# Reordered products, new tiles for exponentials and later operand splits in a softmax-attention and Fourier-mixing kernel

## The chip, the cores and the metric

The kernel runs on 1 core of one Trainium2 chip. The metric is the device time of one execution in microseconds (us); the time before is the median of 3 runs.

## The reference, cut to what matters

One input x of 2048 rows and 512 columns goes through 32-head softmax attention (a head has 16 columns) and through a Fourier mixing layer, and a gate per row mixes the two:

```python
x = A_x                                              # [1, 2048, 512]
g = sigmoid((x * gate_w).sum(-1, keepdims=True))
q, k, v = split(x @ wqkv)                            # 32 heads of 16
p = softmax(q k^T / 4)                               # 2048 x 2048 for each head
a = concat(p @ v) @ wo
re, im = x @ dft_hid_re.T, x @ dft_hid_im.T
b = dft_seq_re @ re - dft_seq_im @ im
out = g * a + (1 - g) * b
```

All inputs and outputs are float32.

## The kernel before, in words

The kernel is one long program whose order is written out by hand: every engine executes its instructions in the order in which the Python code emits them.

**Number formats.** Products that need full precision are made of three single-pass products: an operand is split into a high and a low half (`hi`, `lo`, type float32r), and high x high, high x low and low x high are summed in PSUM. Scores use stacked rows of such halves: a product of 48 or 50 rows holds them all.

**Two halves of the rows.** Nearly all products contract over 64 rows or fewer, so that two run side by side in TensorE, one on rows 0 to 63 (`j = 0`) and one on rows 64 to 127 (`j = 1`). The two heads of a pair lie on the two halves. A product in the lists below is a letter and the half: `e1` is an `e` on rows 64 to 127.

**The front** (to about 345 us) makes q, k, v, the gate and the two halves of the hidden transform (`ab_d`, kept in DRAM), and begins to scan scores for their maxima.

**The main part** is 512 steps, in 256 rounds of two steps. A step belongs to a pair of heads, a half of the queries (1024 columns) and a block of 128 keys. In a round TensorE executes products of four kinds:

- `e` (L633, `score`): a score product into a PSUM bank, read by the exponential on ScalarE (L621, `exponentials`), which writes a tile of 128 x 512 in SBUF. There are 8 in a round.
- `c` (L664, `scan`): a score product of a later pair of heads into a PSUM bank, read by a maximum on VectorE (L666). There are 6 in most rounds.
- `s` (L882, `fill` and `emit`): a filler, one of the products of the Fourier layer's sequence transform (`spectral`), and after it of the output projection (`mix_heads`, `mix_some`). Each half has a bank of its own for them (`z0`, `z1`); when a group of products is complete, VectorE takes it out (L791, L793, L827 `take_in`).
- the weighted values of two earlier steps (L643, `pv`), which use all 128 rows and read 4 exponential tiles per step.

**Order and banks.** `ORDERS` holds the order of the products in a round, by the number of scan pairs and of fillers per half: `(3, 8)` is the usual one. In rounds 0 to 41 (`SINGLES`) there are no fillers, and each half of a round uses `ORDERS[1]`. `e` and `c` share PSUM banks, seven in rounds 0 to 41 and five (`b0` to `b4`) after. Which bank a product gets is decided at build time by the class `Banks`, a small model of the two halves, of ScalarE and of VectorE: it hands out the bank that is free first by its own reckoning. Its constants are in ns.

**Exponential tiles.** There are 17 places of 128 x 512 (`unused`). Before the change they are 17 fixed tiles, 8 of them parts of the `ring4` tiles (named `eb`), 9 of their own (`e`), which are written again and again. `pv` gives the places of its step back.

**Work in the other queues.** VectorE, ScalarE, GpSimd (POOL) and the SP queue of DMAs execute their instructions in order too:

- `split_unit` (L231, L232, POOL) splits a unit of sequence coefficients into `chi` and `clo`, operands of the next 12 fillers of each half.
- `part_b` splits the imaginary part of the hidden transform, one block of 128 rows at a time, into the halves `oh` and `ol` (L928, L929, POOL), and stores them (L933, SP). Two blocks are done in every 16 steps; all are done within the first 128 steps.
- At the end of every 16 steps, `quotients` copies the weighted values out of PSUM (L673, VectorE), and `divide` turns them, in three pieces at later rounds, into halves: `invert` (L683, L684), `spread` (L688) and `scale` (L691 to L699, POOL, into tiles that are also tagged `oh` and `ol`, stored by L706).
- `output_operands` loads and splits the output matrix, one piece at each `next(operands)`: the split is a cast and a subtraction on VectorE (L740, L741).

Of the kernel before, what the change touches and what calls it, by code (L numbers as in the profile page):

```python
# [10 lines left out]
F32 = mybir.dt.float32  # L11
# [7 lines left out]
P = 128  # L19
# [8 lines left out]
VC = DH + 1  # L28
# [31 lines left out]
def build(tc, x, xT, wqkv, wo, wrT, wiT, cr, ci, gate, out):  # L60
    nc = tc.nc
    with ExitStack() as ctx:
# [4 lines left out]
        ring4 = ctx.enter_context(tc.tile_pool(name="ring4", bufs=4, reuse_waits="tile"))  # L67
# [170 lines left out]
        with ExitStack() as px:  # L238
# [125 lines left out]
            if True:  # L364
                wb = px.enter_context(tc.tile_pool(name="wb", bufs=1))
# [195 lines left out]
        with ExitStack() as pa:  # L561
# [23 lines left out]
            class Banks:  # L585

                slot, late, gap, load, group = 230.0, 450.0, 106.0, 200.0, 854.0
                period, release = {"e": 480.0, "c": 680.0}, {"e": 760.0, "c": 860.0}
                names = [f"b{i}" for i in range(5)] + ["z0", "z1"]

                def __init__(self):
                    self.t, self.rows, self.free = 0.0, [0.0, 0.0], [0.0] * 7
                    self.count = 7
                    self.engine, self.values = {"e": 0.0, "c": 0.0}, False

                def take(self, kind, j):
                    if self.values:
                        self.t += self.load
                        self.rows, self.values = [self.t, self.t], False
                    s = max(self.t, self.rows[j])  # L600
                    if kind != "s":
                        b = min(range(self.count), key=lambda b: self.free[b])
                        s = max(s, self.free[b])
                        a = max(self.engine[kind], s + self.late)
                        self.engine[kind], self.free[b] = a + self.period[kind], a + self.release[kind]
                    self.t, self.rows[j] = s + 4.0, s + self.slot
# [503 lines left out]
```

## Time and profile before

| | |
|---|---|
| median of 3 runs | 1775.72 us (1775.24 to 1777.4) |
| the profiled execution's own time | 1774.39 us |
| its span | 1772.6 us, mean clock 0.99 |
| DVE (VectorE) busy | 1259.0 us, 71% |
| ACT (ScalarE) busy | 1328.3 us, 75% |
| POOL (GpSimd) busy | 671.3 us, 38% |
| DMA | 207.01 MB, mean 117 GB/s |

The costliest groups (line, engine, operation, tiles, count; busy us, mean ns) are these:

| group | busy, mean |
|---|---|
| L666 DVE maxima x1312 | 858.0 us, 686 ns |
| L621 ACT exponentials x2048, in two groups | 587.1 and 529.3 us, 638 and 637 ns |
| L633 PE score products x2048 | 685.5 us, 417 ns |
| L882 PE fillers, chi x2060 | 556.2 us, 396 ns |
| L664 PE scan products x1312 | 554.3 us, 456 ns |

Times are those of one profiled execution. PE is TensorE's products, PEld its weight loads. Two products that run side by side are both counted as busy, and so is one that waits for its bank, so that the sums of busy time are larger than the time that TensorE needs. Neighbouring ACT instructions overlap in the trace: their starts are closer together than one lasts. A line of the order of time gives the start, the length, the engine, the line, the operation, the tiles, the shapes and how many instructions were merged; behind it, in brackets, stands the idle time before it and what ended that.

### The profile page before, as it was taken

The page shows a single profiled execution, that of the slowest core. Times are in us where ns is not written, and L with a number is a line of the kernel's source. Part 1 is how long each engine was busy: PE and PEld are TensorE (multiplying, and loading weights), DVE is VectorE, ACT ScalarE, POOL GpSimd, SP SyncE. Part 2 cuts the span into 40 slices and gives each one's busy share as a digit, 9 for nine tenths or more (in the row PEclk, how much of TensorE's full clock was granted, in tenths as well). Part 3 has the DMA queues.
Part 4 walks back from the last instruction along what each step waited for, and adds up shares of the span by engine and source line. Part 5 has one row for each costly group of instructions (what it writes and reads, how often), then busy time and mean ns, then how long its engine had stood idle before and what let it go on. Part 6 is the DMA issues. An engine that isn't in the chain of part 4 may idle for free.

```text
span 1772.6 us, 37250 instructions
## 1 busy us (share of the span) xinstructions
PE 1732.2 (98%) x13657; PEld 1076.3 (61%) x13657; DVE 1259.0 (71%) x2385; ACT 1328.3 (75%) x2589; POOL 671.3 (38%) x828
## 2 busy tenths in 40 slices
PE   8999999999999999999999999999999999999898
PEld 6777788744445565666566665566556656655454
DVE  5599899766676677777777767777777777776334
ACT  5589988799986677777777767677777777777685
POOL 0264210533434544444444444434434444442122
PEclk9999999999999999999999999999999999999999
DMA  7575335763444252333332265524342524426512
GB/s 260 188 235 157 84 118 141 197 174 90 107 108 115 83 144 64 83 96 82 77 93 80 68 180 171 130 63 100 96 100 64 133 58 97 110 58 186 140 42 99
DMA packets 135176, 207.01 MB, mean 117 GB/s; under 512 B 56192, under 2 KB 58736, under 8 KB 130672
## 3 DMA queue, kind: packets, MB, share of 16 engines
q1 hardware_dynamic: 94320, 176.24, 35.6%
q0 software_dynamic: 38496, 19.47, 4.8%
q10 hardware_dynamic: 2176, 8.92, 1.8%
q8 instruction: 107, 1.75, 0.4%
q14 instruction: 77, 0.63, 0.1%
HBM read 138.28 MB, written 65.81 MB: 115 GB/s over the span
## 4 chain that ended last, share of the span: by engine, by line
PE 88%; DMA 4%; issue 2%; DVE 1%; POOL 1%; ACT 1%; SPq 1%; DVEq 0%; POOLq 0%; ACTq 0%
PE pvb L643 26%; PE z L882 23%; PE s L664 12%; PE s L633 12%; PE xy L320 6%; PE s L173 5%; PE xy L336 4%; DMA o_d<-ol 1%; DMA lc<-ob 1%; POOL lc L676 1%; SPq L127 0%; DMA q_d<-el 0%; DMA ks<-k_d 0%; DVE y L827 0%; DVE ob L673 0%
## 5 line engine op out<-in xcount | busy, mean ns | idle before, releaser
L666 DVE TENSOR_REDUCE mx<-s 128x1 f32<-128x512 f32 x1312 | 858.0, 686 | 302.9 <-PE s L633 227.5
L621 ACT ACTIVATE e<-s 128x512 f32<-128x512 f32 x1081 | 587.1, 638 | 182.1 <-PE s L633 167.3
L633 PE MATMUL s<-qs,ks 50*128 50x512 f32 x2048 | 685.5, 417 | 5.1 <-DVE mx L666 4.3
L621 ACT ACTIVATE eb<-s 128x512 f32<-128x512 f32 x967 | 529.3, 637 | 170.2 <-PE s L633 145.2
L882 PE MATMUL z<-b,chi 64*128 64x512 f32 x2060 | 556.2, 396 | 6.2 <-POOL chi L231 6.2
L664 PE MATMUL s<-ks,qs 48*128 48x512 f32 x1312 | 554.3, 456 | 0.0
L633 PEld LDWEIGHTS s<-qs,ks 50*128 50x128 f32 x2048 | 349.1, 186 | 148.9 <-issue 71.2
L643 PE MATMUL pvb<-e,va 128*17 128x512 f32 x2162 | 407.7, 595 | 0.0
L643 PE MATMUL pvb<-eb,va 128*17 128x512 f32 x1934 | 379.6, 597 | 0.0
L882 PEld LDWEIGHTS z<-b,chi 64*128 64x128 f32 x2060 | 342.5, 188 | 36.5 <-POOL chi L231 6.9
L882 PE MATMUL z<-b,clo 64*128 64x512 f32 x1030 | 346.8, 396 | 0.3 <-POOL clo L232 0.3
L664 PEld LDWEIGHTS s<-ks,qs 48*128 48x128 f32 x1312 | 229.3, 185 | 179.4 <-ACT e L621 82.5
L179 DVE CUSTOM_DVE_ANT_0 fold<-s,fold 128x512 f32<-128x512 f32 x368 | 242.7, 689 | 25.3 <-ACT fold L177 8.7
L173 PE MATMUL s<-ks,qs 48*128 48x512 f32 x736 | 231.9, 400 | 1.5 <-ACT fold L177 1.1
L231 POOL CAST chi<-craw 128x512 fp32r<-128x512 f32 x126 | 77.5, 615 | 393.2 <-PE z L882 393.0
L177 ACT ACTIVATE fold<-s 128x512 f32<-128x512 f32 x368 | 203.4, 605 | 28.3 <-PE s L173 27.1
L882 PEld LDWEIGHTS z<-b,clo 64*128 64x128 f32 x1030 | 180.8, 188 | 16.9 <-POOL clo L232 1.6
L232 POOL TENSOR_TENSOR clo<-craw,chi 128x512 fp32r<-128x512 f32 x126 | 162.1, 1286 | 10.7 <-PE z L882 0.3
L676 POOL DMA_DIRECT2D lc<-ob x124 | 63.4, 516 | 251.2 <-DVE ob L673 249.4
L173 PEld LDWEIGHTS s<-ks,qs 48*128 48x128 f32 x736 | 133.8, 184 | 35.8 <-DVE mx L179 12.8
L643 PEld LDWEIGHTS pvb<-e,va 128*17 128x17 f32 x2162 | 70.3, 96 | 112.5 <-issue 111.8
L643 PEld LDWEIGHTS pvb<-eb,va 128*17 128x17 f32 x1934 | 64.8, 96 | 98.5 <-issue 98.0
(129 smaller groups left out, 1756.5 us busy)
## 6 DMA issues: line engine op xcount, KB each, us to landing
craw<-cr SPq DMA_DIRECT2D x64, 256.0 KB
craw<-ci SPq DMA_DIRECT2D x64, 256.0 KB
ks<-k_d SPq DMA_DIRECT2D x54, 256.0 KB
qs<-q_d SPq DMA_DIRECT2D x66, 128.0 KB
ab_d<-ab SPq DMA_DIRECT2D x32, 256.0 KB
y_d<-y SPq DMA_DIRECT2D x32, 256.0 KB
b<-bs_d SPq DMA_DIRECT2D x32, 256.0 KB
o_d<-oh POOLq DMA_DIRECT2D x28, 256.0 KB, 9.5
```

The lines of the kernel that those rows point to most:

```text
L173: nc.tensor.matmul(ps, qs[b:b + 48, qb * P:(qb + 1) * P], ks[b:b + 48, c * 512:(c + 1) * 512], start=True, stop=True)
L177: seen_by(nc.scalar.activation(fold[j], ps, AF.Relu))
L179: seen_by(nc.vector.tensor_tensor_reduce(out=fold[j], in0=ps, in1=fold[j], scale=1.0, scalar=-3.0e38, op0=ALU.add, op1=ALU.max, accum_out= ...
L232: sub(lo, raw, hi.bitcast(F32))
L320: ins = nc.tensor.matmul(ps, lhs[64:P], rhs[64:P], start=False, stop=last)
L621: nc.scalar.activation(e, ps, AF.Exp, scale=SCALE)
L633: nc.tensor.matmul(ps, ks[b:b + 50, kb * P:(kb + 1) * P], qs[b:b + 50, q0:q0 + 512], start=True, stop=True)
L643: nc.tensor.matmul(pvb[r:r + VC, :], va[:, kb, 2 * p + j, :], es[step][c, j], start=kb == 0, stop=kb == NB - 1, tile_position=(0, r))
L664: nc.tensor.matmul(ps, qs[b:b + 48, qb * P:(qb + 1) * P], ks[b:b + 48, c * 512:(c + 1) * 512], start=True, stop=True)
L666: nc.vector.tensor_reduce(mx[p][:, j, qb, c:c + 1], ps, axis=AX.X, op=ALU.max)
L676: nc.gpsimd.dma_start(lc[32 * n:32 * n + 32, :], ob[r + DH:r + VC, :].rearrange("p (s e) -> p s e", e=16))
L882: nc.tensor.matmul(ps, pr_.lhs(j), pr_.rhs(j), start=group.count[j] == 1, stop=group.count[j] == group.size)
```

## The change

The change has five parts.

- Most entries of `ORDERS` have the same products in another order.
- An exponential writes a new tile, taken from the pool `pr` under one of 17 tags, where it wrote one of 17 fixed tiles. The `ring4` pool is closed with the front, and all 17 places lie in `pr`.
- `Banks` has other constants, and its reckoning now has the weight loads (`weights`, one after another through one port) and the swap of weights in each half.
- After the spectral part, each round takes one piece of `output_operands` where it took two.
- In `part_b` a block is split 7 steps after its load where it was 2, and stored 9 steps after it where it was 4; the odd blocks begin one step earlier (3 steps behind the even ones, not 4).

```diff
-    1: "e1 e0 c1 e0 c0 e1",
+    1: "e0 e1 c0 c1 e0 e1",
     0: "e0 e1 e0 e1",
-    (3, 8): "c1 e0 s1 c0 s1 e0 e1 s0 s0 s1 s0 c1 e1 s0 s1 c0 s1 s0 e1 s0 s1 e0 s1 c0 s1 s0 e1 s0 e0 c1",
+    (3, 8): "c0 e1 c0 e1 s0 s1 s0 s1 s0 s1 e0 s1 c0 e1 s1 s0 c1 e0 s1 s0 s1 s0 s0 c1 e1 s0 e0 s1 e0 c1",
...
-    (0, 9): "e1 s0 s1 e0 e1 s0 s1 s0 s1 s0 s1 s0 s1 e0 s1 s0 s1 s0 e1 e0 e1 e0 s1 s0 s1 s0",
-    (0, 6): "e0 e1 e0 s1 s0 s1 s0 s1 s0 e1 e0 e1 s0 s1 e0 s1 s0 s1 s0 e1",
+    (0, 9): "s0 e1 s0 s1 s0 s1 e0 s1 e0 e1 e0 s1 s0 s1 s0 s1 s0 s1 s0 s1 e0 e1 s0 s1 s0 e1",
+    (0, 6): "e0 s1 s0 e1 s0 e1 e0 s1 s0 s1 s0 e1 e0 s1 s0 s1 s0 s1 e0 e1",
...
-        ring4 = ctx.enter_context(tc.tile_pool(name="ring4", bufs=4, reuse_waits="tile"))
...
+                ring4 = px.enter_context(tc.tile_pool(name="ring4", bufs=4, reuse_waits="tile"))
...
-            both = [ring4.tile([P, 2, 512], F32, tag="c", name="eb") for _ in range(4)]
-            unused = [b[:, j, :] for b in both for j in range(2)]
-            unused += [pr.tile([P, 512], F32, name=f"e{i}") for i in range(9)]
+            unused = list(range(17))
...
-                slot, late, gap, load, group = 230.0, 450.0, 106.0, 200.0, 854.0
-                period, release = {"e": 480.0, "c": 680.0}, {"e": 760.0, "c": 860.0}
+                slot, late, gap, load, group, weights, second = 226.0, 425.0, 93.0, 207.0, 854.0, 103.0, 56.0
+                period, release = {"e": 475.0, "c": 682.0}, {"e": 635.0, "c": 735.0}
...
                     if self.values:
-                        self.t += self.load
-                        self.rows, self.values = [self.t, self.t], False
-                    s = max(self.t, self.rows[j])
+                        t = self.t = self.port = self.t + self.load - self.weights
+                        self.rows, self.swap, self.values = [t, t], [t, t + self.second], False
+                    s = max(self.port, self.swap[j])
                     if kind != "s":
                         b = min(range(self.count), key=lambda b: self.free[b])
                         s = max(s, self.free[b])
-                        a = max(self.engine[kind], s + self.late)
-                        self.engine[kind], self.free[b] = a + self.period[kind], a + self.release[kind]
-                    self.t, self.rows[j] = s + 4.0, s + self.slot
-                    return kind != "s" and self.names[b]
+                    self.port = s + self.weights
+                    self.t = self.swap[j] = max(self.port, self.rows[j], self.t + 6.0)
+                    self.rows[j] = self.t + self.slot
+                    if kind == "s":
+                        return None
+                    a = max(self.engine[kind], self.t + self.late)
+                    self.engine[kind], self.free[b] = a + self.period[kind], a + self.release[kind]
+                    return self.names[b]
...
-                    e = es[step][c, j] = unused.pop(0)
+                    i = unused.pop(0)
+                    e = pr.tile([P, 512], F32, tag=f"e{i}", name="e")
+                    es[step][c, j] = e, i
                     nc.scalar.activation(e, ps, AF.Exp, scale=SCALE)
...
-                for s, i in ((2 * s, i), (2 * s + 1, i - 4)):
+                for s, i in ((2 * s, i), (2 * s + 1, i - 3)):
...
-                elif i == 2:
+                elif i == 7:
                     hi, lo = (ap.tile([P, D], F32R, tag=tag, name=tag) for tag in ("oh", "ol"))
...
-                elif i == 4:
+                elif i == 9:
...
                 if m >= OUTM:
-                    for _ in range(2):
-                        next(operands, None)
+                    next(operands, None)
```

More of the change, by code (lines that the diff above doesn't have):

```diff
@@ L585, in build @@
             class Banks:
[L587 to L588 removed]
+                slot, late, gap, load, group, weights, second = 226.0, 425.0, 93.0, 207.0, 854.0, 103.0, 56.0
+                period, release = {"e": 475.0, "c": 682.0}, {"e": 635.0, "c": 735.0}
                 names = [f"b{i}" for i in range(5)] + ["z0", "z1"]
                 def __init__(self):
[L592 to L593 removed]
+                    self.t, self.port, self.rows, self.swap = 0.0, 0.0, [0.0, 0.0], [0.0, 0.0]
+                    self.free, self.count = [0.0] * 7, 7
                     self.engine, self.values = {"e": 0.0, "c": 0.0}, False
@@ L642, in pv @@
                 for c, j, r in quads:
-                    nc.tensor.matmul(pvb[r:r + VC, :], va[:, kb, 2 * p + j, :], es[step][c, j],
+                    nc.tensor.matmul(pvb[r:r + VC, :], va[:, kb, 2 * p + j, :], es[step][c, j][0],
                                      start=kb == 0, stop=kb == NB - 1, tile_position=(0, r))
-                unused.extend(es.pop(step).values())
+                unused.extend(i for e, i in es.pop(step).values())
                 exponentials()
```

4 rows, old and new, of the table ORDERS are left out of this document.

## The prediction

> **What bounds the kernel now.** I read the page first, then the busy time by stage, then single rounds in order of time, and last the waits. The page:
>
> ```profile
> span 1772.6 us, 37250 instructions
> PE 1732.2 (98%) x13657; PEld 1076.3 (61%) x13657; DVE 1259.0 (71%) x2385; ACT 1328.3 (75%) x2589; POOL 671.3 (38%) x828
> PE 88%; DMA 4%; issue 2%; DVE 1%; POOL 1%; ACT 1%; SPq 1%; DVEq 0%; POOLq 0%; ACTq 0%
> ```
>
> TensorE sets the end, but 98% busy does not say that it loses nothing: a product that waits for a bank, beside a running one, still counts as busy. So I go by the length of a round. Exponentials (L621) in the first part (83 half-rounds, rounds 0 to 41) and in the 188 spectral rounds with three scan pairs:
>
> ```profile
> 349.00:512.00 163.00, 162.06 (x332) 0.99 0.48 122
> 524.35:1622.78 1098.43, 781.03 (x1504) 1.00 0.38 98
> ```
>
> The columns are window, length, ACT busy (count), clock. 332 / 4 is 83 half-rounds of 1.96 us, with ScalarE busy 99%: ScalarE is the bound there. 1504 / 8 is 188 rounds of 5.84 us, with ScalarE at 71%: there it is TensorE. One of these (864 to 870), PEld its weight loads:
>
> ```profile
> 863.92 0.49 PE L664 MATMUL s<-ks,qs 48*128 48x512 f32 x1
> 863.93 0.49 PE L633 MATMUL s<-qs,ks 50*128 50x512 f32 x1
> 864.26 0.39 PE L882 MATMUL z<-b,chi 64*128 64x512 f32 x1
> 864.49 0.40 PE L882 MATMUL z<-b,clo 64*128 64x512 f32 x1
> 865.20 0.18 PEld L664 LDWEIGHTS s<-ks,qs 48*128 48x128 f32 x1
> 865.69 0.18 PEld L664 LDWEIGHTS s<-ks,qs 48*128 48x128 f32 x1
> 866.67 0.18 PEld L664 LDWEIGHTS s<-ks,qs 48*128 48x128 f32 x1
> 867.37 0.18 PEld L633 LDWEIGHTS s<-qs,ks 50*128 50x128 f32 x1 [0.17 <-ACT e L621]
> 867.48 0.39 PE L633 MATMUL s<-qs,ks 50*128 50x512 f32 x1
> 867.80 0.62 PE L643 MATMUL pvb<-eb,va 128*17 128x512 f32 x4
> 869.64 0.18 PEld L664 LDWEIGHTS s<-ks,qs 48*128 48x128 f32 x1 [0.85 <-ACT eb L621]
> 864.55 0.60 ACT L621 ACTIVATE e<-s 128x512 f32<-128x512 f32 x1 [1.48 <-PE s L633]
> 865.04 0.59 ACT L621 ACTIVATE e<-s 128x512 f32<-128x512 f32 x1
> 866.23 0.39 PE L633 MATMUL s<-qs,ks 50*128 50x512 f32 x1
> 866.72 0.60 ACT L621 ACTIVATE e<-s 128x512 f32<-128x512 f32 x1
> 864.46 2.56 DVE L666 TENSOR_REDUCE mx<-s 128x1 f32<-128x512 f32 x4 [1.54 <-PE s L633]
> ```
>
> A round is 15 pairs (one product on each half of the rows) and then two steps of weighted values. The first gap between pairs is 0.34, later ones 0.23 (864.26 to 864.49). Free of waits the last pair starts at 0.34 + 13 x 0.231 = 3.34; here the last product starts at 867.48 - 863.92 = 3.56. So 0.22 of this 5.72 us round are waits, and four weight loads show for what: 865.20, 865.69 and 867.37 stand 0.05 behind the end of an exponential (864.55 + 0.60, 865.04 + 0.59, 866.72 + 0.60), 866.67 behind one between them. They wait for a bank that ScalarE still reads. That is the room of the new orders: 0.22 x 188 = 41 us at most. The other 0.12 of the mean 5.84 is a few long waits, below.
>
> **The orders.** I redo the round with the new order, from the rows' constants: an exponential starts 0.62 after the round's first pair, later 0.49 after its product (866.23 to 866.72) or the one before it (864.55 to 865.04), and its bank takes weights 0.65 after that start. A reduction starts 0.54 after the first pair, else 0.61 after the one before ((2.56 - 0.69) / 3), and frees its bank 0.69 later. Weights lead their product by 0.10 (867.37 to 867.48). The new order has c0 e1, c0 e1, three pairs of fillers, e0 s1 (at 1.26), c0 e1 (1.49), fillers, c1 e0 (1.96), two of fillers, then c1 (2.65), e1 (2.88), e0 (3.11) and e0 c1 (3.34). The first five take empty banks. Exponentials free theirs at 1.27, 1.76, 2.40, 2.89, 3.38; reductions at 1.23, 1.84, 2.72, 3.33. In turn: c0 and e1 at 1.49 take 1.23 and 1.27; c1 and e0 at 1.96 take 1.76 and 1.84; c1 at 2.65 takes 2.40; e1 at 2.88 takes 2.72 (its 0.10 of weights fit); e0 at 3.11 takes 2.89; the last pair takes 3.33 and 3.38 and starts at 3.48. Four waits become one: 3.56 - 3.48 = 0.08 a round, 15 us over 188. Where the plan hands out the last two banks in the other order, the end is the same, since both are in one pair. The rounds with nine fillers a side or fewer have no waits to lose: they are 5.05 apart (below), which is 5.72 - 0.22 less two slots.
>
> **New tiles for exponentials.** One line, and four exponentials of the bound first part:
>
> ```profile
> L621 ACTq EVENT_SEMAPHORE  x1031: 17/17/17, 352.0 to 1624.3; - x172
> 426.10 1.35 ACT L621 ACTIVATE eb<-s 128x512 f32<-128x512 f32 x2
> 426.61 0.84 ACT L621 ACTIVATE eb<-s 128x512 f32<-128x512 f32 x1
> 427.10 0.84 ACT L621 ACTIVATE e<-s 128x512 f32<-128x512 f32 x1
> 427.58 1.34 ACT L621 ACTIVATE e<-s 128x512 f32<-128x512 f32 x2
> 428.06 1.35 ACT L621 ACTIVATE e<-s 128x512 f32<-128x512 f32 x2
> ```
>
> Half of the 2048 exponentials have a second wait as an instruction of its own. By the code it is ScalarE's own count, beside TensorE's, because the fixed tile was written by an earlier exponential. Starts stand 0.51, 0.49, 0.48, 0.48 apart: around that wait 0.04 more than two plain ones. A new tile in an old place should wait for its last reader only, which is TensorE again, so one wait is left. In the first part a half-round then takes 4 x 0.48 = 1.92 instead of 163 / 83 = 1.964: 83 x 0.045 = 3.7 us. TensorE's own need there lies below it: before ScalarE is full, half-rounds take 1.88 (from 355.65 to 357.53), so at most 0.08 x 83 = 6.6 us could come, and at least nothing.
>
> ```profile
> 355.65 0.19 PEld L633 LDWEIGHTS s<-qs,ks 50*128 50x128 f32 x2 [0.85 <-issue]
> 357.53 0.19 PEld L633 LDWEIGHTS s<-qs,ks 50*128 50x128 f32 x2 [0.85 <-issue]
> ```
>
> In the spectral rounds each exponential that waits starts about 0.05 earlier (in the first pair the reduction starts after 0.54, the exponential after 0.62). Then the last pair takes 3.33 at worst and starts at 3.43: 0.13 a round instead of 0.08, 188 x 0.13 = 24.4 us. Bounds: 0, where the plan's banks miss, and 41. The Trainium skill (Perfetto Trace Analysis, Identifying Dependency Chains) says that an instruction that waits for several engines may get such a wait put before it. If the second wait were another engine's, a new tile would remove nothing; that is a rival below, and by it the sum is 13 us smaller.
>
> **Output operands.** Rounds after the spectral part, and what DVE did:
>
> ```profile
> 1644.43:1652.80 8.37, 0.81 (x7) 0.49 (x5) 3.15 (x5) 0.60 (x1) 3.64 (x3) 0.82 0.57 105
> 1652.80:1659.42 6.62, 6.62 (x43) 3.82 (x41) 3.22 (x5) 3.75 (x7) 0.00 (x0) 0.71 0.02 4
> 1659.42:1664.47 5.05, 5.05 (x48) 2.79 (x44) 1.50 (x2) 4.13 (x8) 0.00 (x0) 1.00 0.51 110
> 1649.48 0.43 DVE L740 CAST b<-wor 128x512 fp32r<-128x512 f32 x1 [10.17 <-DMA wor<-wo]
> PE z L882 <- DVE y L827: 8.2, 2, 7.6
> ```
>
> The first two lines are one round of 14.99 us; the next takes 5.05. DVE stood 10.17 us in a cast (L740) whose operand had not landed, and behind it the take_in (L827) that frees the z bank. Now the cast is asked for one round after the loads; with one part per round it is two rounds later, 2 x 5.05 = 10.1 us, against the 10.17. Without the stall the operand lands at 1649.5 in the round that starts near 1648.3, and the take_in queued behind is due only at that round's end, 1653: covered. 14.99 - 5.05 = 9.9 us gained; bounds 0 and 10. What else is later (the last split, three rounds) has more than ten rounds before its first use. The clock in the second line (0.71) is part of the price. The Trainium skill (TensorE: Matmul & The Clock Gate, Part 1) has the clock halved after an idle window and restored after 3.4 us busy; by it the stall costs 7.6 + 1.7 = 9.3, the sum 0.6 less. The trace agrees: 9.9, with 0.71 in the round's second half.
>
> **Coefficient halves later.** POOL splits them (L928), in the same queue as the split of the filler's operands (L231):
>
> ```profile
> 518.73 0.86 POOL L706 DMA_DIRECT2D o_d<-oh  x1
> 528.64 0.61 POOL L928 CAST oh<-braw 128x512 fp32r<-128x512 f32 x1 [8.23 <-DMA o_d<-oh]
> 576.11 0.61 POOL L928 CAST oh<-braw 128x512 fp32r<-128x512 f32 x1 [5.18 <-DMA o_d<-oh]
> 530.07:539.91 9.84, 7.71 (x50) 4.33 (x46) 4.12 (x6) 4.45 (x8) 7.46 (x10) 0.83 0.38 122
> 568.79:575.14 6.35, 6.18 (x52) 3.37 (x48) 3.96 (x6) 4.29 (x8) 2.06 (x3) 1.00 0.40 97
> 575.14:586.83 11.69, 7.42 (x52) 4.06 (x48) 3.95 (x6) 4.24 (x8) 7.49 (x10) 0.85 0.27 88
> ```
>
> Against 5.72 these three rounds lose 4.1 + 0.6 + 6.0 = 10.7 us: POOL waits for the store of the quotients' halves to land (9.9 us after issue at 518.73) because both use tile oh, and the filler's split comes late. Only the last steps of this work fall into spectral rounds. Later, the split no longer stands ahead of the quotients' scaling, so that store is issued 2 to 5 us earlier, and the first stall (4.1) goes; the second split meets the landing about 3 us less early. New is a wait at the period's end: the odd half's bs_d store (SP queue) is issued in the very macro in which the scaling asks for oh; POOL stands there some 4 us, with L231 queued behind it. The filler's split has about 1.4 rounds, 8 us, of slack, which covers one such wait and not two. I take +6, bounds -8 and +10.7.
>
> **The sum.** 24.4 + 3.7 + 9.9 + 6 = 44 us. The profiled execution takes 1774.4 (1772.6 span); it would be 1730.4. The median of the runs is 1775.7, 1.3 above it: **1731.7**.
>
> **The rivals.** (1) The second wait stays: rounds gain 0.08, the first part nothing: 15 + 9.9 + 6 = 31, 1744.8. For it: the profile's rows do not name what the wait is for. 0.10. (2) The later splits collide with the scaling: -8 instead of +6, 1745.7. For it: POOL's new wait of 4 us; against: only three periods. 0.08. (3) The orders gain nothing, since banks are handed out by planned times: 19.6 is left, 1756. 0.09. (4) **Slower**: the plan now reckons a bank free 0.425 + 0.635 = 1.06 after an exponential's product, the rows show 0.49 + 0.65 = 1.14 and more. If a product at the round's end is given a bank whose exponential is one further back in the queue, it waits 0.48 more: last pair at 3.91, 0.35 over now, +66 us in all, less the other 19.6: 1822. It decides against the change from 0.10 a round lost on (19.6 / 188). Against it: the hand count has each bank free in the order that the plan assumes. 0.08. The forecast has 0.62; the last 0.03 are gains and losses that cancel.
>
> **How the numbers follow.** A measurement of this kernel can tell about 0.2% (3.6 us). Faster: 0.62 + 0.10 + 0.08 + 0.09 = 0.89, same 0.03, slower 0.08. The range takes in the rivals up to (3), and below the forecast all waits of a round gone (41) with 3.7, 9.9 and 10.7: 65 us, 1710. So 1710 to 1757.
>
> **What would show it.** Right: 1504 exponentials of the spectral rounds in about 1065 us, half-rounds of 1.92, no L621 event semaphores, no long wait of L740, rounds near 1650 of 5.05. Wrong: weight loads still behind exponentials three or four times a round, the event semaphores still there, or new POOL waits in L698 with TensorE behind L231 near 585 and 620.

## The result and the profile after

The changed kernel takes 1753.74 us, the median of 4 runs (1749.17 to 1757.9), against 1775.5 of the kernel before on the same chip (1775.24 to 1777.4): a ratio of 0.9875 (0.9848 to 0.9901). That is 22 us, half of the 44 forecast. The profiled execution took 1752.48 us. Its page, with the lines that answer to those of before:

```profile
span 1750.7 us, 36734 instructions
PE 1717.3 (98%) x13657; PEld 1028.3 (59%) x13657; DVE 1257.5 (72%) x2385; ACT 1346.2 (77%) x2589; POOL 669.9 (38%) x828
PE 81%; DMA 6%; issue 3%; POOL 3%; DVE 2%; SPq 1%; ACT 0%; DVEq 0%; POOLq 0%; ACTq 0%
```

DMA and POOL have grown in the chain that ended last (the work that sets the end, followed back step by step), from 4% to 6% and from 1% to 3%. That is a first hint that TensorE now waits more for data; the rounds below show where. (In this kernel the exponential is L625, the score product L637, the weighted values L647, the scan L668, its maximum L670, the filler L886, its operand's split L230.)

A usual spectral round of it, 872.31 to 877.92, by its score and scan products, the weight load that shows a wait, and the start of the next round:

```profile
872.31 0.49 PE L668 MATMUL s<-ks,qs 48*128 48x512 f32 x1
872.64 0.39 PE L668 MATMUL s<-ks,qs 48*128 48x512 f32 x1
873.58 0.40 PE L637 MATMUL s<-qs,ks 50*128 50x512 f32 x1
873.82 0.39 PE L668 MATMUL s<-ks,qs 48*128 48x512 f32 x1
874.28 0.39 PE L668 MATMUL s<-ks,qs 48*128 48x512 f32 x1
874.98 0.39 PE L668 MATMUL s<-ks,qs 48*128 48x512 f32 x1
875.21 0.39 PE L637 MATMUL s<-qs,ks 50*128 50x512 f32 x1
875.45 0.39 PE L637 MATMUL s<-qs,ks 50*128 50x512 f32 x1
875.64 0.18 PEld L637 LDWEIGHTS s<-qs,ks 50*128 50x128 f32 x1 [0.23 <-ACT e L625]
875.68 0.47 PE L668 MATMUL s<-ks,qs 48*128 48x512 f32 x1
876.08 1.91 PE L647 MATMUL pvb<-e,va 128*17 128x512 f32 x16
877.92 0.50 PE L668 MATMUL s<-ks,qs 48*128 48x512 f32 x1
```

The hand count of the new order had pairs at 1.26, 1.49, 1.96, 2.65, 2.88, 3.11 and the last at 3.43. They stand at 1.27, 1.51, 1.97, 2.67, 2.90, 3.14 and 3.37 behind 872.31. One weight load of the last pair still stands behind an exponential, and the round has next to no wait left. The stages tell what became of it. These are the windows of after for the exponentials of the spectral rounds, and for the rounds around the three longest waits (window, length, the five engines busy, clock, DMA share, GB/s; the first line has ACT alone):

```profile
524.70:1611.30 1086.60, 800.55 (x1504) 0.99 0.38 100
...
570.30:582.30 12.00, 9.23 (x52) 4.36 (x48) 4.05 (x6) 4.45 (x8) 9.34 (x12) 0.72 0.37 122
644.30:655.90 11.60, 8.64 (x50) 5.60 (x46) 4.15 (x6) 4.46 (x8) 1.89 (x2) 0.71 0.64 143
1013.90:1024.60 10.70, 7.55 (x50) 5.20 (x46) 4.15 (x6) 4.46 (x8) 0.00 (x0) 0.84 0.77 181
1646.40:1651.50 5.10, 5.10 (x50) 2.85 (x46) 2.58 (x5) 4.16 (x10) 0.00 (x0) 1.00 0.74 155
```

The 188 rounds take 1086.6 us and not 1098.4. Three of them take 10.7 to 12 us. After the spectral part a round near 1650 takes 5.1; the 14.99 us round is gone.

By stage, from the first products of the rounds (a median round is the median of their distances):

| stage | before | after |
|---|---|---|
| rounds 0 to 41, 83 half-rounds | 166.7 us | 165.7 us |
| the half-round there, median | 1.960 us | 1.960 us |
| rounds 44 to 63 | 125.8 us | 119.7 us |
| rounds 64 to 231 | 972.7 us | 967.0 us |
| median round of these | 5.732 us | 5.611 us |
| rounds 234 to 249 | 92.8 us | 82.6 us |

So 1.0 + 6.1 + 5.7 + 10.2 = 23 us are in these stages. (The first 1.0 is no gain: the first score product comes at 346.64 and not at 345.58.) The median round gained 0.121 us, which would be 20.3 us over the 168 rounds from 64 on; 5.7 came. The question is where the other 14.6 went.

### The profile page after: what moved, and what is told of

The parts are those of the page before. It is cut to its first block, busy times and chain, and to the rows that moved or that the text cites. A ratio compares the mean times of both kernels' runs of the same rounds, so it can differ in the third digit from the quotient of the medians.

```text
span 1750.7 us, 36734 instructions
## 1 busy us (share of the span) xinstructions
PE 1717.3 (98%) x13657; PEld 1028.3 (59%) x13657; DVE 1257.5 (72%) x2385; ACT 1346.2 (77%) x2589; POOL 669.9 (38%) x828
## 4 chain that ended last, share of the span: by engine, by line
PE 81%; DMA 6%; issue 3%; POOL 3%; DVE 2%; SPq 1%; ACT 0%; DVEq 0%; POOLq 0%; ACTq 0%
PE pvb L647 25%; PE z L886 20%; PE s L668 14%; PE s L637 12%; PE xy L319 4%; PE s L172 4%; PE xy L335 3%; POOL el L261 1%; DMA lc<-ob 1%; SPq L126 1%; DMA ks<-k_d 1%; DMA o_d<-ol 1%; DMA qs<-q_d 1%; DMA qs<-m_d 1%; POOL eh L261 1%
## 5 line engine op out<-in xcount | busy, mean ns | idle before, releaser
L625 ACT ACTIVATE e<-s 128x512 f32<-128x512 f32 x2048 | 1072.0, 638 | 311.3 <-PE s L637 271.0
L670 DVE TENSOR_REDUCE mx<-s 128x1 f32<-128x512 f32 x1312 | 853.8, 686 | 290.7 <-PE s L637 193.2
L637 PE MATMUL s<-qs,ks 50*128 50x512 f32 x2048 | 656.0, 426 | 8.3 <-DMA qs<-q_d 3.2
L647 PE MATMUL pvb<-e,va 128*17 128x512 f32 x4096 | 501.8, 597 | 0.0
L668 PE MATMUL s<-ks,qs 48*128 48x512 f32 x1312 | 488.1, 420 | 2.1 <-DVE mx L670 1.9
L886 PE MATMUL z<-b,chi 64*128 64x512 f32 x2060 | 484.9, 394 | 1.9 <-POOL chi L230 1.9
L637 PEld LDWEIGHTS s<-qs,ks 50*128 50x128 f32 x2048 | 327.0, 185 | 153.9 <-issue 76.4
L668 PEld LDWEIGHTS s<-ks,qs 48*128 48x128 f32 x1312 | 214.7, 186 | 193.2 <-issue 128.0
L886 PE MATMUL z<-b,clo 64*128 64x512 f32 x1030 | 304.7, 395 | 0.9 <-POOL clo L231 0.9
L886 PEld LDWEIGHTS z<-b,chi 64*128 64x128 f32 x2060 | 288.3, 187 | 27.2 <-POOL chi L230 2.3
L172 PE MATMUL s<-ks,qs 48*128 48x512 f32 x736 | 235.6, 401 | 1.6 <-ACT fold L176 1.2
L176 ACT ACTIVATE fold<-s 128x512 f32<-128x512 f32 x368 | 202.9, 604 | 28.9 <-PE s L172 27.4
L230 POOL CAST chi<-craw 128x512 fp32r<-128x512 f32 x126 | 77.2, 613 | 380.5 <-PE z L886 358.8
L647 PEld LDWEIGHTS pvb<-e,va 128*17 128x17 f32 x4096 | 93.4, 96 | 216.0 <-issue 214.8
L886 PEld LDWEIGHTS z<-b,clo 64*128 64x128 f32 x1030 | 160.1, 188 | 15.1 <-POOL clo L231 1.2
L231 POOL TENSOR_TENSOR clo<-craw,chi 128x512 fp32r<-128x512 f32 x126 | 161.8, 1284 | 10.5
L335 PE MATMUL xy<-w,b 64*128 64x512 f32 x384 | 121.1, 400 | 0.0
L319 PE MATMUL xy<-w,b 64*128 64x512 f32 x384 | 117.1, 392 | 0.0
L319 PEld LDWEIGHTS xy<-w,b 64*128 64x128 f32 x384 | 71.7, 187 | 7.9 <-DVE mx L178 0.6
```

What stands on the lines that cost most here:

```text
L172: nc.tensor.matmul(ps, qs[b:b + 48, qb * P:(qb + 1) * P], ks[b:b + 48, c * 512:(c + 1) * 512], start=True, stop=True)
L176: seen_by(nc.scalar.activation(fold[j], ps, AF.Relu))
L231: sub(lo, raw, hi.bitcast(F32))
L319: ins = nc.tensor.matmul(ps, lhs[64:P], rhs[64:P], start=False, stop=last)
L335: nc.tensor.matmul(ps, lhs[0:64], rhs[0:64], start=n == 0, stop=False)
L625: nc.scalar.activation(e, ps, AF.Exp, scale=SCALE)
```

## Where the gain went

First, rounds 64 and 128, the first of a pair of heads. What waits in round 64:

```profile
PEld s L637 <- issue: 3.2, 1, 3.2
PE s L637 <- DMA craw<-cr: 3.0, 1, 3.0
```

The first `e1` waits 3 us, put down to a transfer that came last by the profile; the product reads only the rows of its pair. Those rows are loaded by the SP queue. Its issues ahead of round 64, before (which reaches that round at 650.1) and then after (644.3):

```profile
633.71 2.39 SPq L127 DMA_DIRECT2D ks<-k_d  x4
640.80 6.29 SPq L127 DMA_DIRECT2D qs<-q_d  x8
```

```profile
629.89 2.39 SPq L126 DMA_DIRECT2D ks<-k_d  x4
636.26 6.35 SPq L126 DMA_DIRECT2D qs<-q_d  x8
```

Before, the loads begin 16.4 us ahead of the round, after only 14.4. By the program they can begin when the last scan of the pair that gives up the slot has run, and that is the first `c1` of round 61. The old order had `c1` first in the round, the new one has its first `c1` in place 16, 1.97 us in. That is the 2 us (an experiment below moves this scan alone). Round 128 waits 3.2 us for its q rows too, but there the loads begin 11.1 us ahead in both kernels (1007.77 to 1018.9 before, 1002.80 to 1013.9 after): another cause, found below. Behind both waits the granted clock is low. The windows of round 64 cut finer:

```profile
644.30:647.70 3.40, 0.53 (x5) 0.18 (x1) 0.69 (x1) 0.00 (x0) 0.00 (x0) 0.85 0.36 128
647.70:651.10 3.40, 3.31 (x16) 2.87 (x18) 1.03 (x2) 1.68 (x3) 0.69 (x2) 0.50 0.86 210
651.10:653.20 2.10, 2.10 (x14) 1.76 (x12) 1.04 (x2) 1.20 (x2) 1.19 (x1) 0.50 1.01 176
653.20:655.90 2.70, 2.70 (x23) 0.78 (x19) 1.38 (x2) 1.57 (x3) 0.00 (x0) 0.94 0.45 51
```

The mean clocks say how long it stood at half: 0.15 / 0.5 x 3.40 = 1.0 us at the end of the first stretch, the two middle ones whole (5.5 us) and 0.06 / 0.5 x 2.70 = 0.3 us of the last, 6.8 us in all, from 646.7 on. So 5.8 us behind the wait ran at half speed, which costs 2.9 us; with the 3.0 us of the wait that is 5.9 of the 6.0 lost. In round 128 the clock stood at half for 3.4 us (mean clocks of 0.68 and 0.83 over the 3.40 and 3.70 us behind the wait): 3.2 + 1.7 = 4.9 of the 5.1. The Trainium skill (TensorE: Matmul & The Clock Gate, Part 1) says that the clock is halved after an idle window of about 3.4 us, is restored after a busy one, and that these windows run freely. The lengths agree, since 3.4 and 6.8 us are one and two such windows. That the window must be idle as a whole this trace does not bear out: the last product before the wait ended at 644.83 (644.33 + 0.50), and the clock fell 1.9 us later.

Second, VectorE. The new order has both its first scans in the first two pairs, `c0 e1 c0 e1`, when VectorE may be at something else. Round 105 of after, in which it copies the weighted values (L677):

```profile
883.76 0.69 DVE L677 COPY ob<-pvb 128x512 f32<-128x512 f32 x1 [1.25 <-PE pvb L647]
884.36 1.28 DVE L670 TENSOR_REDUCE mx<-s 128x1 f32<-128x512 f32 x2
885.10 0.18 PEld L668 LDWEIGHTS s<-ks,qs 48*128 48x128 f32 x1 [0.32 <-DVE mx L670]
```

The first maximum starts 0.81 after its product (883.55) instead of 0.54, and the weights of the third scan wait 0.32 for its bank. The 21 rounds behind a copy take 5.827 us, 0.216 over the median; before it was 5.769, 0.037 over. That is 21 x 0.18 = 3.8 us. In 28 rounds VectorE takes out a group of fillers: there the excess grew from nothing to about 0.09, 2.6 us.

Third, round 216 loses 1.9 us because a y tile lands late, and rounds 84 and 190 lose 1.4 together. The list from round 64 on is 7.8 (rounds 64 and 128, which lost 3.3 before), 3.8, 2.6, 1.9 and 1.4: 17.5, of which 0.9 came back in the rounds two behind a copy. That is 2 us more than the 14.6 to be explained. Some of it is counted twice: of the 28 rounds behind a take-out, seven are also two behind a copy, and one is round 84.

Fourth, the coefficient halves. POOL around round 52 (570.3) of after:

```profile
559.35 0.86 POOL L710 DMA_DIRECT2D o_d<-oh  x1
568.69 0.60 POOL L932 CAST oh<-braw 128x512 fp32r<-128x512 f32 x1 [5.13 <-DMA o_d<-oh]
572.22 1.26 POOL L933 TENSOR_TENSOR ol<-braw,oh 128x512 fp32r<-128x512 f32 x1 [2.93 <-DMA o_d<-ol]
573.43 0.60 POOL L230 CAST chi<-craw 128x512 fp32r<-128x512 f32 x1
```

The wait of round 45 (4.1 us) is gone. In round 52 the split still waits for the store of the quotients' halves, 5.1 and 2.9 us, with the filler's split (L230) behind it: 6.4 us lost, 6.0 before.

## The experiments: each part by itself

**New tiles alone** (the kernel before, with an exponential writing a new tile under one of 17 tags).

```diff
-                    e = es[step][c, j] = unused.pop(0)
+                    i = unused.pop(0)
+                    e = pr.tile([P, 512], F32, tag=f"e{i}", name="e")
+                    es[step][c, j] = e, i
```

> The kernel before with one change: exponentials write new tiles in 17 places, old orders, old reckoning of banks. Theory: an exponential that finds ScalarE idle starts about 0.06 us earlier, and the median three-scan round goes from 5.73 to about 5.65 us; the first part stays at 1.96 us a half-round, since ScalarE's own pace of 0.49 us an exponential sets it: 13 to 17 us less. Rival (the prediction's): the first part falls to 1.92 as well, 4 us more. Second rival: without the new orders the earlier starts only move the waits, under 5 us.

1776.32 us against 1776.34, ratio 0.9997 (0.9985 to 1.0009): nothing, where 13 to 17 us were expected. The second waits of the whole execution, in this kernel and then in the changed one:

```profile
L621 ACTq EVENT_SEMAPHORE  x1031: 17/17/17, 353.0 to 1626.4; - x172
```

```profile
L625 ACTq EVENT_SEMAPHORE  x545: 17/17/17, 352.2 to 1612.8; - x182
```

All 1031 stand as before. By the program, a new tile in an old place waits for its last reader and its last writer just as the fixed tile did. The profile doesn't name what the wait is for; but the counts worked out in this way ahead of two runs below (191 and 269) were met (192 and 270). What decides on the wait is the sequence in which places are written and given back, and the orders set that.

**The orders alone** (with the new `Banks`).

```diff
-    (3, 8): "c1 e0 s1 c0 s1 e0 e1 s0 s0 s1 s0 c1 e1 s0 s1 c0 s1 s0 e1 s0 s1 e0 s1 c0 s1 s0 e1 s0 e0 c1",
+    (3, 8): "c0 e1 c0 e1 s0 s1 s0 s1 s0 s1 e0 s1 c0 e1 s1 s0 c1 e0 s1 s0 s1 s0 s0 c1 e1 s0 e0 s1 e0 c1",
```

> The kernel before with one change: the new orders and the new reckoning of banks, fixed exponential tiles. Theory: the median three-scan round goes from 5.73 to about 5.65 (15 us over 188), but rounds that begin with VectorE busy (the 21 copies of weighted values, the takings of finished groups) lose 0.1 to 0.2 us each, and the row loads for the pairs that begin near 650 and 1019 us come late (4 to 8 us): 2 to 8 us less in all. Rival: the median gain comes through whole, 15 us less.

1769.48 us (1766.88 to 1773.76), ratio 0.9964 (0.9948 to 0.9979): 6.9 us less, within the 2 to 8 expected. The median round is 5.611 (5.65 expected) and there are 545 second waits, both as in the changed kernel: all of the shorter round, and all of the fewer waits, come with the orders and their reckoning of banks, which were not run apart. Round 64 loses 5.7, so this wait is theirs as well. Round 128 loses 4.3; with the old orders it lost 1.3 to 3.6 in five kernels.

**Output operands alone** (one piece a round).

```diff
-                    for _ in range(2):
-                        next(operands, None)
+                    next(operands, None)
```

> The kernel before with one change: one part of the output operands per round instead of two. Theory: the wait of VectorE's cast for its operand (10.2 us) finds the operand landed two rounds later, and the round near 1645 us shrinks from 14.99 to 5.05 us: 9.9 us less in all, nothing else moves. Rival: the loads are late because of what stands ahead of them in the SP queue, and the cast still waits for some of it: under 5 us less.

1764.8 us (1762.17 to 1766.62), ratio 0.9929 (0.9903 to 0.9955): 11.5 us. Rounds 234 to 249 take 82.3 us, 10.5 less, and nothing else takes the place of the wait.

**Coefficient halves alone.**

```diff
-                elif i == 2:
+                elif i == 7:
...
-                elif i == 4:
+                elif i == 9:
```

> The kernel before with one change: the coefficient halves are split and stored later. Theory: the 4.1 us stall near 530 us goes, the one near 575 us (6.6 us) stays within 1 us, since the split still meets the same landing of the quotients' store: 4 us less. Rival: the store of the odd half and the scaling collide and a new stall of 3 to 8 us comes near 590 or 625.

1767.39 us (1765.65 to 1769.06), ratio 0.9948 (0.9931 to 0.9965). That is 9.0 us by the medians, where 4 were expected. The profiled execution (1769.06) shows 5.1 of them in rounds 44 to 63 (120.7): the 4.1 of round 45 are gone, round 52 still loses 5.4. Where the rest lies was not settled.

The four parts make 0.0 + 6.9 + 11.5 + 9.0 = 27.4 us by themselves, against 21.8 together. By the intervals above the two sums are uncertain by some 7 and 5 us, so this difference is not clear of the noise.

## The experiments: what the second wait costs

**Places in reverse** (the kernel before, where a step gives back its four places in reverse).

```diff
-                unused.extend(es.pop(step).values())
+                unused.extend(reversed(list(es.pop(step).values())))
```

> The kernel before with one change: pv gives the places of a step back in reverse, so that an exponential finds ScalarE's earlier write covered by a wait that went before: 191 instead of 1030 exponentials have the second wait, none of them in the first part. Orders, banks and tiles are as before. Theory: the second wait costs time only where ScalarE is idle before the exponential (start 0.48 us after the product with it, 0.42 without), so the median three-scan round falls from 5.73 to about 5.65 us (15 us over 188), and the first part stays at 1.96 us a half-round. Rival (the prediction's step): the second wait also sets the pace of the first part, which falls to 1.92, 3.7 us more. Second rival: nothing changes, the gain of the orders is theirs alone.

1767.18 us (1764.89 to 1768.1), ratio 0.9948 (0.9933 to 0.9963). That is 8.3 us less, where 15 were expected. 192 second waits are left, and one of them lies in the first part. Exponentials in the same 149.94 us of the first part, in the kernel before, in the changed kernel and in this one, each with its second waits in that window where there are any:

```profile
360.00:509.94 149.94, 149.94 (x308) 1.00 0.47 116
L621 ACTq EVENT_SEMAPHORE  x76: 17/17/17, 361.8 to 508.9; - x76
```

```profile
360.00:509.94 149.94, 149.94 (x307) 1.00 0.47 119
L625 ACTq EVENT_SEMAPHORE  x154: 17/17/17, 360.0 to 509.5; - x154
```

```profile
360.00:509.94 149.94, 149.94 (x308) 1.00 0.47 119
```

With 76, 154 and no second waits ScalarE does 307 or 308 exponentials, one in 0.487 us. On a full ScalarE the wait costs nothing. In the spectral rounds, where ScalarE idles, the median round fell from 5.732 to 5.688 us (5.65 expected) with some four waits fewer: 0.01 us each in this kernel. (In a later kernel one wait fewer a round changed nothing, as the run with reversed places below shows.) The Trainium skill (ScalarE: Activation LUTs, What ACT_TABLE_LOAD costs) makes an activation 186 ns + 0.833 ns for each of 512 elements, less an overlap of 93 ns: an estimate of 0.519. The traces have 0.487, and that decides. ScalarE itself is the pace of that part, and no wait is.

## The experiments: rows, stores and tiles

These start from the changed kernel. The table has what single rounds lost over the median, in us, in the profiled executions.

| round | 52 | 64 | 128 | 194 | 216 | 234 | two behind a copy, 21 rounds |
|---|---|---|---|---|---|---|---|
| before | 6.0 | 0.0 | 3.3 | 0.0 | 0.0 | 0.7 | 5.3 |
| changed | 6.4 | 6.0 | 5.1 | 0.0 | 1.9 | 1.1 | 4.4 |
| scans alternate | 4.0 | 1.4 | 5.8 | 0.1 | 0.1 | 0.6 | 4.2 |
| mirrored | 4.2 | 1.7 | 3.8 | 0.1 | 0.1 | 2.2 | 6.6 |
| own tiles | 0.0 | 3.3 | 2.4 | 0.0 | 6.6 | 1.6 | 5.1 |
| q rows first | 5.8 | 0.9 | 5.9 | 3.7 | 0.9 | 1.6 | 10.5 |
| own, q rows, y early | 0.0 | 0.7 | 4.6 | 0.5 | 0.1 | 1.6 | 6.1 |
| the same, reversed | 0.0 | 0.4 | 4.1 | 1.8 | 0.1 | 1.0 | 8.3 |
| all, and two moves | 0.0 | 0.4 | 1.8 | 0.0 | 0.1 | 12.2 | 1.3 |

**Scans that alternate between the halves**, so that a pair's last scan comes in the second place of its round.

```diff
-    (3, 8): "c0 e1 c0 e1 s0 s1 s0 s1 s0 s1 e0 s1 c0 e1 s1 s0 c1 e0 s1 s0 s1 s0 s0 c1 e1 s0 e0 s1 e0 c1",
+    (3, 8): "c0 e1 c1 e0 s0 s1 s0 s1 s0 s1 s0 e1 c0 e1 s1 s0 c1 e0 s1 s0 s1 s0 s1 c0 e1 s0 s1 e0 e0 c1",
```

> The changed kernel with one change: in the three-scan order the scan products alternate between the halves (c0 e1 c1 e0 ... instead of c0 e1 c0 e1 ..., first c1 at place 2, not 16), kinds at the same places. Theory: the scan that ends a pair of heads is then complete 1.6 us earlier in its round, the SP queue starts the row loads for the next pair that much earlier, and the waits at rounds 64 and 128 (6.0 and 5.1 us) fall to about 2 us each: 6 us less. Against it: three of eight exponentials have a second wait instead of two, up to 0.03 us a round, 5 us. Rival: the row loads are late for another reason, and rounds 64 and 128 stay.

1749.44 us (1747.25 to 1751.68), ratio 0.9846 (0.9829 to 0.9863). Ahead of round 64, which starts at 645.01 here:

```profile
628.76 2.38 SPq L126 DMA_DIRECT2D ks<-k_d  x4
```

The loads begin 16.2 us ahead again, and the round loses 1.4 and not 6.0: the place of the last scan sets their start. Round 128 keeps its wait, against the expectation. The median round rose to 5.638, which is 4.5 us over 168 rounds and the risk that the expectation had named. The time fell by 4.3 us and not by 6.

**The same with the halves exchanged** (`c1 e0 c0 e1 ...`), so that the first score product is on the half whose rows are loaded first.

> The changed kernel with the alternating order mirrored (c1 e0 c0 e1 ...): the first exponential's product uses the rows of half 0, which are loaded first. Theory: as with the alternating order, and the first product of rounds 64 and 128 finds its rows about 1 us earlier still: 7 us less than the changed kernel, rounds 64 and 128 within 1.5 us of the others. Rival: the same as the alternating order, if both halves' rows come late together.

1752.03 us (1745.44 to 1755.8), ratio 0.986 (0.9832 to 0.9888): no different from the one above by these intervals. Rounds 64 and 128 lost 1.7 and 3.8, where at most 1.5 was expected. If it matters which half comes first, these four runs, spread over 10 us, can't tell.

**Coefficient halves in tiles of their own** (an exponential place less).

```diff
-            unused = list(range(17))
+            unused = list(range(16))
...
-                    hi, lo = (ap.tile([P, D], F32R, tag=tag, name=tag) for tag in ("oh", "ol"))
+                    hi, lo = (ap.tile([P, D], F32R, tag=tag, name=tag) for tag in ("bh", "bl"))
```

> The changed kernel with one change: the coefficient halves get tiles of their own (bh, bl) instead of sharing oh and ol with the scaling of the quotients; one place for exponentials fewer (16) makes the room. Theory: POOL no longer waits at L932 and L933 for the store of the quotients' halves (5.1 and 2.9 us near 570 us), the filler's split is in time and the round near 570 us falls from 12.0 to about 5.7 us: 6 us less, nothing else. Rival: the round is late because of the filler's own loads, and stays.

1746.49 us (1746.4 to 1748.12), ratio 0.9835 (0.9821 to 0.985). Round 52 is clean and rounds 44 to 63 take 113.4 us, 6.3 less: the shared tile was the cause, and a 17th place is not needed. But round 216 went from 1.9 to 6.6. What waited in it:

```profile
DVE mx L670 <- PE s L637: 4.6, 3, 1.5
DVE y L797 <- DMA y<-y_d: 4.2, 1, 4.2
```

VectorE stands in the take-out of a group whose y tile has not landed; its load is behind 18 loads of rows in the SP queue and, by that queue's waits, stood 4.0 us more until one of them had landed. It was issued at 1506.53, 2.1 us ahead of the round; in the changed kernel it was 7.1 us (1512.19 to 1519.3), in the kernel before 12.7 (1518.11 to 1530.8).

Round 64 of this kernel shows what the clock adds. Its first `e1` waited 2.9 us, as long as in the changed kernel (3.0), but the round lost 3.3 and not 6.0, for the clock stayed up:

```profile
639.22:642.60 3.38, 0.50 (x7) 0.22 (x3) 0.69 (x1) 0.00 (x0) 0.00 (x0) 1.00 0.38 128
642.60:646.00 3.40, 3.40 (x29) 3.21 (x29) 2.38 (x4) 2.60 (x6) 1.87 (x2) 1.00 0.84 215
```

So rounds 64 and 128 of two kernels can differ by some 3 us without any difference in the wait.

**q rows first**: when a pair's rows are loaded for use, the q rows of the first 1024 queries go ahead of the rows of maxima (m_d).

```diff
-            for load in loads[0]:
+            for load in loads[0] + loads[1]:
                 load()
...
-            for load in loads[1] + loads[2]:
+            for load in loads[2]:
```

> The changed kernel, but when the rows of a pair are loaded for use, the q rows of the first 1024 queries are issued before the rows of maxima (m_d) instead of after them. Theory A: rounds 64 and 128 of the changed kernel wait 6.0 and 5.1 us because the q rows are last in SP's queue, behind m_d rows that wait for the maxima. Then round 64 loses under 1 us (its q rows would be issued by 636, 8 us ahead of 644), round 128 about 2 (its m_d rows are issued until 1012.8, 1.1 before its start, and need about 2 to land), and the time is 7 to 9 us below the changed kernel's 1753.7: 1745 to 1747. Theory B: what lands last are the maxima, or the transfers as a whole are late: then both rounds keep their waits and the time stays within 2 us of 1753.7.

1754.5 us (1753.59 to 1757.26), ratio 0.9879 (0.9864 to 0.9893): no gain over the changed kernel. Theory A was right for round 64 (0.9 lost, under 1 expected) and wrong for round 128 (5.9, about 2 expected). Ahead of that round, SP in this kernel:

```profile
997.72 0.33 SPq L800 DMA_DIRECT2D y_d<-y  x1
998.10 3.93 SPq L126 DMA_DIRECT2D ks<-k_d  x4
1009.38 1.17 SPq L144 DMA_DIRECT2D qs<-m_d  x2
```

```profile
SPq L800 <- DVE y L797: 7.4, 1, 7.4
```

SP stood 7.4 us in the store of a y tile that VectorE had not finished, with all row loads behind it (in the changed kernel 7.4 us too); they begin only at 998.1, 11.1 us ahead of the round (1009.2), where round 64 has 14.4. And the 5.1 us won in round 64 went elsewhere: round 194 lost 3.7, the rounds two behind a copy 10.5 where it was 4.4. What waited in round 194:

```profile
POOL r_d L688 <- DVE lc L687: 3.8, 1, 3.8
DVE lc L687 <- DMA lc<-ob: 3.7, 1, 3.7
PEld s L668 <- DVE mx L670: 2.4, 1, 2.4
```

VectorE waits for the small transfers of the sums (lc), POOL for VectorE, and the scan's bank for the maximum queued on VectorE. Why these transfers landed later in this kernel than in the changed one was not settled.

**Own tiles, q rows first, and the y tile of the second phase fetched four blocks earlier.**

```diff
-                            if s == NB // 2 and i == 0:
+                            if s == NB // (4 if ph else 2) and i == 0:
```

> As a_q, with the coefficient halves in tiles of their own and 16 exponential places (as in a_own), and with the y tile of the second spectral phase fetched four blocks earlier, so that its load is not behind the row loads of round 216. Theory A, the stalls are separate and add: from a_own's 1746.5 go 6.6 at round 216, 3 at round 64 and 0 to 1 at round 128: 1736 to 1738. Theory B, one wait is only the first of several that end close together (row loads, maxima, y load, quotients): some other wait takes its place and the time stays above 1742.

1741.58 us (1737.78 to 1746.95; the profiled execution was the slowest), ratio 0.9796 (0.9777 to 0.9815): the lowest median here, 34 us below the kernel before. It lies between the two theories: rounds 64 and 216 are clean, round 128 lost 4.6 where 1.4 to 2.4 was hoped for.

**The same with places given back in reverse.**

> As a_own_q, with the four exponential places of a step given back in reverse order, which by the program leaves 269 second waits of exponentials where 545 were, one a spectral round instead of two. Theory A, each second wait costs on ScalarE's idle side what it did in the kernel before (0.045 us a round for four of them): 0.01 a round, 2 us in all below a_own_q. Theory B, the second waits that are left out are those before banks that nobody needs yet: median round and time as a_own_q's within 1 us. Either way the first part keeps 1.96 us a half-round.

1742.06 us (1739.47 to 1743.52), ratio 0.9804 (0.979 to 0.9819). 270 second waits instead of 546, a median round of 5.607 instead of 5.608: theory B, the waits left out cost nothing here. The first part keeps 1.960.

**Row loads ahead of the y store, and the division a round later.**

```diff
-                for f in staged.pop(m, ()):
-                    f()
...
                 prefetch(m)
+                for f in staged.pop(m, ()):
+                    f()
...
-(2, 4, 6) if p < NP - 1
+(3, 5, 7) if p < NP - 1
```

> As a_own_q, with two more moves: the row loads of a pair are issued ahead of the store of a finished y tile and not behind it, and the three pieces of the division run 3, 5 and 7 rounds after the copy and not 2, 4 and 6. Theory A: round 128 loses 4.6 us in a_own_q because SP stands 7 us in the store of y (which waits for VectorE) with the row loads behind it; with the loads ahead they start some 4 us earlier and the round loses at most 1. The rounds two after a copy (50, 98, 138, 146, 170, 194) lose 0.5 to 1.3 us each, 5.5 in all, because GpSimd's queue waits for the reciprocal, and that for the four small transfers of the sums, with the split of the coefficients behind it; a round later the transfers have landed. Together 8 to 10 us below a_own_q's 1741.6: 1732 to 1734. Theory B, the work moved collides with the next thing in its queue (the y store a few us late holds its buffer, the scaling lands on the next copy): one of the two gains is lost and the time is 1737 or more.

1748.55 us (1746.32 to 1752.98), ratio 0.9854 (0.9837 to 0.9871): 7 us above the kernel without the two moves. (The profiled executions differ by 0.6 only: that of the kernel without the moves was its slowest, and its round 44 starts 5.4 us later.) Yet both did nearly what theory A said. Round 128 lost 1.8 (at most 1 expected): with the loads 14.8 us ahead (986.69 to 1001.5) its wait fell from 2.7 to 1.4 us. The clock stayed up besides, where it had stood at 0.50 for 3.4 us without the moves, which is some 1.7 of the 2.8 us won. The rounds two behind a copy lost 1.3 in all, and rounds 64 to 231 take 952.8 us against 960.5. Theory B was right too, at one place, round 234 (1601.3 to 1618.6):

```profile
DVE wor L731 <- DMA y_d<-y: 14.0, 1, 14.0
PEld z L886 <- DVE y L831: 12.5, 1, 12.5
```

```profile
1613.98 0.37 SPq L800 DMA_DIRECT2D y_d<-y  x1
```

The last y store is now behind the row loads, at 1613.98. The tile `wor` takes the place of that y, so VectorE stands 14.0 us in its memset (L731), and the take-out that frees the z bank behind it. Rounds 234 and 235 lose 14.8 us, more than both moves won. The kernel without the moves lost 1.6 there. So with the swap made only up to round 233 some 13 us should come back, an estimate of 1735 us by this sum; that was not run.

## The prediction, point by point

**Orders: the mechanism held, the term was too small, and the sum over the rounds did not hold.** The hand count gave the orders by themselves 0.08 us a round, with the last pair at 3.48. By themselves they brought 0.121, with the last pair at 3.39 (medians). That this is near the 0.13 forecast (3.43) for orders and tiles together is luck in part: two errors cancel. A likely reason, not shown by a run of its own, is that the orders also took away three of the five second waits of a spectral round (1031 and 545 in all, of which 80 and 160 lie in the first part). At 0.011 us each, as in the kernel before with its places in reverse, that is an estimate of 0.03.

The failed step is the multiplication by 188. It took the few long waits as fixed, and the waits of the kernel before do not show what is nearly late: rows that landed just in time for round 64, y tiles in time for round 216. It also counted the new order with VectorE idle at the start of each round, which is wrong in some 49 rounds. Of rivals (3), banks handed out by planned times, and (4), the slower one, the median round shows nothing: the last pair starts within 0.05 us of a round free of waits (3.39 against 3.34).

**New tiles: wrong.** Forecast were 3.7 us in the first part and 0.05 of each round; the tiles by themselves did nothing. Two steps failed. That a new tile waits only for its reader: 1031 second waits stood unchanged. And that 0.04 us around such a wait is its cost: with none at all in those 149.94 us the pace was the same 0.487. Rival (1), the second wait stays, was half right: the wait stayed with the new tiles, and half of the waits went with the orders, which the prediction did not see.

**Output operands: right.** 9.9 forecast, 10.2 in the stage; by itself 10.5 in the stage and 11.5 by the medians.

**Coefficient halves: the sign held, the size is open.** Forecast were 6 us. By itself the part brought 9.0 by the medians (6.2 to 12.3 by the interval) but 5.1 in the stage; in the changed kernel rounds 45 and 52 together won 3.7. The first stall (4.1) went, as forecast. The failed step is that the second split would meet the landing about 3 us less early: POOL waits 5.1 and 2.9 us there and the round loses 6.4, against 5.2 and 3.1 and 6.0 before the change. The new collision with the scaling that rival (2) priced did not show: POOL waited 0.5 us for `bs_d` near 583.

**The sum.** Of the 44 us, 3.7 never were there (tiles in the first part). Of the 24.4 in the spectral rounds 22.7 came (0.121 x 188), but 14.6 of them went into new waits. Of the 6 of the coefficient halves 3.7 came. That leaves 22. The time came out inside the range only because the range reached to the rivals: 1753.7 lies next to rival (3)'s 1756, whose mechanism did not occur, so that much is luck. One of the signs to look for did not follow from the prediction's own sum either: it says 1065 us for the spectral rounds, where 1098.4 - 24.4 - 6 makes 1068. They took 1086.6.

## What to carry to other kernels

A saving per round, times the rounds, is an upper bound: when the rounds get shorter or their order moves a last use, everything that was just in time behind them (row loads, stores that hold a queue, tiles that are reused) can become the next wait, and one wait of 3 us cost 6.0 in one kernel here and 3.3 in another, by what the clock did. So before such a change list, for each queue, how far ahead of its need each load lands, and look at what an in-order queue stands in front of. A wait that is an instruction of its own cost nothing here on a full engine, and little or nothing on an engine that idles; measure the pace of the full engine before pricing it.

## What was not expected of the hardware

A second wait on a full ScalarE cost nothing (308 exponentials in 149.94 us with 76 of them or with none), on an idling one about 0.01 us of the round in one kernel and nothing in another. With a wait of 3.0 us the granted clock stood at 0.50 for 6.8 us, and a late load cost twice its lateness; with a wait of 2.9 us in another kernel it stayed at 1.00. The changed kernel's four runs spread over 8.7 us, those of the kernel before beside it over 2.2; but 17 runs of the kernel before on another chip spread over 8.5 too (1773.48 to 1781.94).
